# Loading a kernel's first activations by column blocks instead of row blocks

## The chip, the cores and the metric

The kernel runs on one core of a Trainium2 chip. The metric is the device time of one execution in microseconds, as the median of several runs. The core has TensorE (PE), VectorE (DVE), ScalarE (ACT), GpSimd (POOL) and SyncE (SP), and 16 DMA engines. SyncE and ScalarE each issue DMAs on a queue of their own; the 16 engines serve both queues.

## What is computed

The input `x` has 2048 rows of 448 columns in bfloat16. Two branches run over it and are mixed row by row with a gate:

```
g = sigmoid(sum(x * gate_w))                       # one number for each row
a = 2 * Re(C h) + x * Dskip,  h_t = Lam_bar h_(t-1) + B_bar x_t     # a diagonal state-space scan, 448 complex states
b = silu(x @ w1) @ w2                              # w1 is 448 x 1792, w2 is 1792 x 448
out = g * a + (1 - g) * b
```

## The kernel before

**Layout.** Two rows of `x` are taken as one row of 896 values, `x2` (1024 x 896): columns 0 to 447 are the even rows, 448 to 895 the odd ones. TensorE needs `x` with its columns on the partitions; that is `XT`. Columns 0-127, 128-255 and 256-383 fill three column blocks j = 0, 1, 2 of 128 partitions. The remainder, columns 384-447, is half a block (j = 3), and the upper half of the matching tile `XR` holds a second copy of it, so that two matmuls of 64 partitions can run side by side. W1 lies in `W1E` in the same way: row blocks j = 0, 1, 2 and a remainder of 64 rows, `W1E[.., 3, ..]`. This text calls the row blocks W1 block 0, 1 and 2.

**The head.** Nearly all of `XT` is made by transposing DMAs on SyncE's queue, which come late. To start sooner, the first 512 even rows (four row blocks k = 0 to 3 of 128 rows, 512 columns each) come by plain loads into `XH` (a view of `XN`) and are transposed by TensorE: `turn_k(j, k)` (L488) transposes one block of 128 x 128 into PSUM, `turned_k` (L498) and `turned_x` (L504) copy one or several from PSUM into `XT` on VectorE. With them `ffn1_first` (L430) works on the first six blocks of 128 columns of W1: for j = 0, 1, 2 in turn it adds W1's block j times `XT`'s block j into six PSUM banks. Block j = 0 is done in two halves of 256 columns (h = 0 for row blocks 0 and 1, h = 1 for 2 and 3), j = 1 and 2 in one piece of 512. `ffn1_first` is a generator: at each `yield` the code that drives it puts transposes between its matmuls. After it the remainder j = 3 follows (`ffn1_rem`, L444), then silu on ScalarE (L452), and from there the long steady part (`pair`, `lanes`, L362), which runs through the rest of both branches.

**What sets the order.** Every engine runs its instructions in the order of the program. `Tracker` puts a wait before an instruction for each buffer it reads or writes that another engine or a DMA has not finished; the names in `reads` and `writes` are these buffers. A DMA counts as landed when all 16 of its parts have landed. Loads go by `ld` (L226), on the queue of the engine that is named. The first loads are, in order:

- SyncE: row block 0, columns 0-255 (`XA0`); half of W1 block 0; row block 2, columns 0-383 (`XA2`); W1 block 1; two rows for the scan's coefficients (`log_dt`, `Lambda_re`); columns 384-511 of row blocks 2 and 3 (`XB1`); then W1's remainder and its further columns.
- ScalarE: row block 1, columns 0-255 (`XA1`); the other half of W1 block 0; row block 3, columns 0-383 (`XA3`); columns 256-511 of row blocks 0 and 1 (`XB0`); `Lambda_im`; W1 block 2; a table load; then W1's remainder and its further columns.

SyncE then waits for both pieces of W1's remainder (`gE`) before it issues the transposing DMAs. While the head runs, the three rows of coefficients are transposed by four small matmuls (`mm_cols`, L469) and go through a chain of small operations on VectorE and ScalarE; the copies of block j = 3 into `XT` (L504) and `XR` (L568) stand behind the first links of that chain on VectorE.

TensorE begins with 20 matmuls on a constant (`warm`, L478).

Of the kernel before, what the change touches and what calls it, by code (L numbers as in the profile page):

```python
# [11 lines left out]
BF16 = DT.bfloat16  # L12
# [138 lines left out]
def gated_mix(nc, A_x, A_Lambda_re, A_Lambda_im, A_B_re, A_B_im, A_C_re, A_C_im, A_log_dt,  # L151
              A_Dskip, B_x, B_w1, B_w2, gate_w, out):
    with ExitStack() as ctx:
        E = ctx.enter_context
        T = Tracker(nc, ctx)

        def sb(name, shape, dtype):
            return E(nc.sbuf_tensor(name, list(shape), dtype))
# [4 lines left out]
        XT = sb("XT", [128, 8, NK], BF16)  # L163
# [7 lines left out]
        XR = sb("XR", [128, NK], BF16)  # L171
# [17 lines left out]
        ID = sb("ID", [128, 128], BF16)  # L189
# [31 lines left out]
        ps = E(nc.psum_tensor("ps", [128, 8, 512], F32))  # L221
# [3 lines left out]
        def ld(eng, dst, src, key, group=None):  # L225
            return T.dma(eng, lambda e: e.dma_start(dst, src), writes=[key], group=group)  # L226
# [2 lines left out]
            return T.dma("sp", lambda e: e.dma_start_transpose(dst, src), reads=reads,  # L229
                         writes=[key, *also], group=group)  # L230

        XE = [(["XTe000", "XTe001", "XTe010", "XTe011", "XTe02"], ["XTe03"]), (["XTe1"], ["XTer1"])]
        XO = [([f"XTo{h}"], [f"XTr{h}"]) for h in range(2)]

        def swap_xr(eng, h, odd):
# [4 lines left out]
            else:  # L240
                T.op(eng, lambda e: e.tensor_copy(XR[64:128, hs], XT[0:64, 3, hs]), reads=XE[h][1],
                     writes=[f"XR{h}a"])
# [8 lines left out]
            return v.rearrange("(o n) -> o n", o=1)  # L251

        XH = XN[:, 0:8 * D].rearrange("p (k c) -> p k c", k=4)
        XA = ["XA0", "XA1", "XA2", "XA3", "XB0", "XB1"]
        FA, FB = 768, 1280
        x0 = x2[0:512, 0:512].rearrange("(k p) c -> p k c", p=128)

        def ld_w(eng, j, f0=0, f1=FA, key=""):
            ld(eng, W1E[:, j, f0:f1], B_w1[j * 128:(j + 1) * 128, f0:f1], f"W1Ej{j}{key}")

        def ld_row(eng, i, v):
            ld(eng, R[i:i + 1, 0:D], row(v), f"R{i}", gR if i < 2 else gR2)
# [9 lines left out]
                          B_w1[384:448, FA:].rearrange("p (n c f) -> p n c f", n=2, c=2)[:, :, c, :], f"W1Es{c}")  # L272
            return ld(eng, W1E[p, 3, 0:384], B_w1[384:448, 384 * c:384 * c + 384], f"W1Er{c}")

        for k, eng in enumerate(("sp", "act")):
            ld(eng, XH[:, k, 0:256], x0[:, k, 0:256], XA[k])
        for c, eng in enumerate(("sp", "act")):
            ld_w(eng, 0, 384 * c, 384 * c + 384, c)
        for k, eng in ((2, "sp"), (3, "act")):
            ld(eng, XH[:, k, 0:384], x0[:, k, 0:384], XA[k])  # L280
        ld_w("sp", 1)
        ld("act", XH[:, 0:2, 256:512], x0[:, 0:2, 256:512], XA[4])
        for i, (eng, v) in enumerate((("sp", A_log_dt), ("sp", A_Lambda_re), ("act", A_Lambda_im))):
            ld_row(eng, i, v)
        ld_w("act", 2)
        ld("sp", XH[:, 2:4, 384:512], x0[:, 2:4, 384:512], XA[5])
        T.op("act", lambda e: e.activation(JK[:, 0:1], HP[:, :], AF.Exp), reads=["HP"], writes=["JK0"])
        gE = [ld_wr(eng, c, False) for c, eng in enumerate(("sp", "act"))]
        ld_w3("sp", 0, 2, FA, FB, "d")
# [20 lines left out]
        for i, src in enumerate((A_B_re, A_B_im)):  # L310
# [15 lines left out]
             writes=["IOTA"])  # L326
# [9 lines left out]
        def nxt():  # L336
            n_bank[0] += 1
            return BANKS[(n_bank[0] - 1) % len(BANKS)]
# [7 lines left out]
        def rem_keys(odd, h, p):  # L346
            return (XO if odd else XE)[h][1] if (p is UP) == bool(odd) else [f"XR{h}{'b' if odd else 'a'}"]

# [48 lines left out]
        def ff(fb):  # L397
            i, c = fb // 2, fb % 2
            return i + 3 * c if i < 3 else i + 3 + 2 * c if i < 5 else i + 5 + 2 * c

        def wj(fb):
            i, c = fb // 2, fb % 2
            return [f"W1Ej0{c}", "W1Ej1", "W1Ej2"] if i < 3 else ["W1Ed0", "W1Ed2"] if i < 5 else ["W1Ee0", "W1Ee1"]

        def w1(fb):
            return lambda p, j: W1E[p, j, ff(fb) * 128:(ff(fb) + 1) * 128] if j < 3 else \
                W1E[p, j, fb // 2 * 128:(fb // 2 + 1) * 128]

        def rem_ffn1(odd, h, fb):
            return [*[f"W1E{'r' if fb < 6 else 's'}{c}" for c in range(2)], *rem_keys(odd, h, LO), *rem_keys(odd, h, UP)]  # L410
# [6 lines left out]
        def ffn1_pair(c, fb, p=None):  # L417
            odd, h = c // 2, c % 2
            banks = at(p) if p is not None else [nxt(), nxt()]
            return (*[(banks[i], odd, h, w1(fb + i)) for i in range(2)],  # L420
                    wj(fb) + wj(fb + 1) + (XO if odd else XE)[h][0], rem_ffn1(odd, h, fb),
                    lambda: ffn1_act(c, fb, banks[0], 2))

        def ffn1_first():
            banks = [nxt() for _ in range(NF1)]
            for j, h in ((0, 0), (0, 1), (1, None), (2, None)):
                c = slice(0, 512) if h is None else slice(256 * h, 256 * h + 256)
                for n, fb in enumerate((0, 2, 4, 1, 3, 5)):
                    bank = banks[fb]
                    T.op("pe", lambda pe, fb=fb, bank=bank, j=j, h=h, c=c: pe.matmul(  # L430
                        ps[:, bank, c], W1E[:, j, ff(fb) * 128:(ff(fb) + 1) * 128], XT[:, j, c],
                        start=(h == 0), stop=(h == 0), skip_group_check=(h != 0)),
                        reads=[f"W1Ej{j}" if j else f"W1Ej0{fb % 2}"] + (
                            ["XTe02"] if j == 2 else [f"XTe0{j}{h}"] if h is not None else [f"XTe0{j}0", f"XTe0{j}1"]),
                        writes=[f"ps{bank}"])
                    if (j, h, n) in ((0, 0, 3), (0, 0, 5), (1, None, 2), (1, None, 5)):
                        yield
            yield banks

# [10 lines left out]
        def ffn1_act(c, fb, bank, n=1):  # L450
            a = AT[c % 2]
            T.op("act", lambda e: e.activation(a[:, fb:fb + n, :], ps[:, bank:bank + n, :], AF.Silu),  # L452
                 reads=[f"ps{bank + i}" for i in range(n)], writes=[f"AT{c % 2}_{fb + i}" for i in range(n)])
# [26 lines left out]
            T.op("pe", mm, writes=[f"ps{b}"])  # L480

        warm(NWARM, 5)
        PB = (6, 7, 6, 7)
        xp = [ps[:, b, 0:256].bitcast(BF16) for b in PB]

        def turn_k(j, k, b=None):
            b = PB[j] if b is None else b
            T.op("pe", lambda pe: pe.transpose(  # L488
                ps[:, b, 0:256].bitcast(BF16)[:, k * 128:(k + 1) * 128], XH[:, k, j * 128:(j + 1) * 128], ID[:, :]),
                reads=[XA[k if j < 2 or (j == 2 and k > 1) else 4 + k // 2], "ID"], writes=[f"ps{b}"])  # L490

        def turn_x(j, i):
            for k in (2 * i, 2 * i + 1):
                turn_k(j, k)

        def turned_k(j, k, b):
            c = slice(128 * k, 128 * k + 128)
            T.op("dve", lambda e: e.tensor_copy(XT[:, j, c], ps[:, b, 0:256].bitcast(BF16)[:, c]),  # L498
                 reads=[f"ps{b}"], writes=[f"XTe0{j}{k // 2}" + ("" if k % 2 else "a")])

        def turned_x(j, i=None, b=None):
            c, key = (slice(0, 512), f"XTe0{j}") if i is None else (slice(256 * i, 256 * i + 256), f"XTe0{j}{i}")
            b = PB[j] if b is None else b
            T.op("dve", lambda e: e.tensor_copy(XT[:, j, c], ps[:, b, 0:256].bitcast(BF16)[:, c]),  # L504
                 reads=[f"ps{b}"], writes=[key])

        for k in range(2):
            turn_k(0, k, 6 - k)
            turned_k(0, k, 6 - k)
        turn_x(1, 0)  # L510
        turned_x(1, 0)
        warm(2, 4)
        first = ffn1_first()
        next(first)
        for k in (2, 3):
            turn_k(0, k, k + 4)
            turned_k(0, k, k + 4)
        next(first)
        for k in (2, 3):
            turn_k(1, k, 6)  # L520
        turned_x(1, 1, 6)
        rd()
        next(first)
        T.op("pe", mm_cols, reads=["R0", "R1", "R2", "Rd", "ID"], writes=["pv"])
        T.op("dve", lambda e: e.tensor_copy(
            PV[:, :, :], ps[:, 7, 256:288].rearrange("p (t c) -> p t c", c=8)[:, :, 0:4]),
            reads=["pv", "ps7"], writes=["PV"])
        for i in range(2):
            turn_x(2, i)
        turned_x(2)  # L530
        next(first)
        for i in range(2):
            turn_x(3, i)
# [24 lines left out]
        def pact(o, a, f, ra, scale=1.0, bias=0.0):  # L558
# [6 lines left out]
        ptt("ar", col("dt"), LRE, ALU.mult, ["dt", "PV"])  # L565
        pact("mag", col("ar"), AF.Exp, ["ar"])
        turned_x(3)
        T.op("dve", lambda e: e.tensor_copy(XR[64:128, 0:512], xp[3][0:64, :]), reads=["ps7"], writes=["XR0a"])  # L568
        T.op("act", lambda e: e.activation(JK[:, 0:1], HP[:, :], AF.Silu), reads=["HP"], writes=["JK0"])
        ld_b(GWB, gate_w, "GW")  # L570
        ld_b(DB, A_Dskip, "DB")
# [9 lines left out]
            reads=["f2"] + SGN, writes=["f2s"])  # L581
# [55 lines left out]
        def xblock(b):  # L637
            v = XN[:, 4 * b * D:4 * (b + 1) * D].rearrange("p (k c) -> p k c", k=4) if b > 1 else \
                XH[:, :, b * D:(b + 1) * D]
            return v, [*(XA if b < 2 else []), *([f"XN{b // 2}"] if b else [])]  # L640

# [24 lines left out]
        for n in (32, 64):  # L666
            T.op("dve", lambda e, n=n: e.tensor_copy(GD[n:2 * n, :, :], GD[0:n, :, :]), reads=["GW", "DB"],
                 writes=["GW", "DB"])
# [7 lines left out]
             writes=["BTz"] + BTK[2:4])  # L676
# [174 lines left out]
        def bu_even(pt, h, p=None, q=None):  # L851
# [4 lines left out]
            def done():  # L856
# [5 lines left out]

            return (*[(b[i], 0, h, lambda p, j, i=i: bt(p, j, m + i)) for i in range(2)], BTK[0:2] + XE[h][0],
                    BTK + XE[h][0] + rem_keys(0, h, LO) + rem_keys(0, h, UP), done)

# [5 lines left out]
        def bu3_even(p, q):  # L871
            b = at(p)

            def done():
# [7 lines left out]

            return (*[(b[h], 0, h, lambda p, j: bt(p, j, 6)) for h in range(2)], ["BR"] + XE[0][0] + XE[1][0],
                    ["BR"] + rem_keys(0, 0, LO) + rem_keys(0, 1, UP), done)
# [278 lines left out]
        f = ffn1(2)  # L1163
# [100 lines left out]
```

## Time and profile before

| | before |
|---|---|
| runs, us | 136.57, 136.66, 136.79 (median 136.66) |
| profiled execution, span from first to last instruction, us | 135.2 |
| the same execution's whole time | not given by the page; the median of the runs is 1.46 us above the span |
| TensorE matmul busy | 131.8 us, 97% |
| VectorE, ScalarE, GpSimd busy | 115.6, 93.8, 15.9 us |
| granted TensorE clock | 1.000 |
| DMA moved | 11.78 MB, most of it in the first third |

In the chain of work that ended last, TensorE has 94% of the span. Matmuls are pipelined and their ends are modelled, so starts are the better marks. An engine that sits idle costs time only where that chain passes through it.

### The profile page before, as it was taken

Reading aid. Unit: us, or ns where it says so; the run is one execution under the profiler, and the core shown is the slowest. Engines: PE = TensorE matmul, PEld = TensorE weight load, DVE = VectorE, ACT = ScalarE, POOL = GpSimd, SP = SyncE. Lnnn points to the kernel's source line nnn. Section 1 sums busy time; section 2 is a strip of 40 time slices with the busy share of each in tenths; the row PEclk is TensorE's granted clock in tenths of the full one; section 3 lists DMA queues with packets and bytes.
Section 4 is the critical chain, followed back from the end, with each engine's and each line's share of the span. In section 5 each row is a group of like instructions: output and inputs, shape, how many; then the busy total and the mean of one; then the engine's idle time right before and its main releaser. Section 6 shows DMA issues by size and latency. Waiting matters only on the chain.

```text
span 135.2 us, 2632 instructions
## 1 busy us (share of the span) xinstructions
PE 131.8 (97%) x1072; PEld 65.4 (48%) x1073; DVE 115.6 (86%) x154; ACT 93.8 (69%) x146; POOL 15.9 (12%) x32
## 2 busy tenths in 40 slices
PE   7899999999999999999999999999999999999993
PEld 7444444444444554444445544445555555555552
DVE  1369999917899798999999999999999999994554
ACT  0459888899939999769999597797114437879200
POOL 7108349650000000000000000000000000000000
DMA  4999979898997220000222000000000000322123
GB/s 110 259 275 176 125 140 264 165 323 248 259 188 119 53 63 0 0 0 0 55 47 58 5 0 0 0 5 0 0 0 0 0 0 5 102 91 79 68 80 124
DMA packets 24736, 11.78 MB, mean 87 GB/s; under 512 B 16851, under 2 KB 24214, under 8 KB 24726
## 3 DMA queue, kind: packets, MB, share of 16 engines
q1 hardware_dynamic: 22996, 10.43, 33.4%
q10 hardware_dynamic: 1730, 1.20, 3.1%
q8 instruction: 8, 0.13, 0.4%
q14 instruction: 2, 0.02, 0.0%
HBM read 5.34 MB, written 1.84 MB: 53 GB/s over the span
## 4 chain that ended last, share of the span: by engine, by line
PE 94%; DMA 2%; DVE 1%; SPq 1%; issue 0%
PE ps L362 44%; PE ps L796 16%; PE ps L811 16%; PE ps L1049 15%; PE ps L430 3%; DMA XN<-in_A_x_dram 2%; PE ps L488 1%; DVE TMPS L1073 1%; SPq L226 1%; PE ps L444 1%; PE ps L469 0%
## 5 line engine op out<-in xcount | busy, mean ns | idle before, releaser
L362 PE MATMUL ps<-XT,W1E 64*128 64x512 bf16 x325 | 41.3, 376 | 0.0
L452 ACT ACTIVATE AT<-ps 128x1024 bf16<-128x1024 f32 x28 | 28.2, 1020 | 7.4 <-PE ps L362 7.2
L362 PEld LDWEIGHTS ps<-XT,W1E 64*128 64x128 bf16 x325 | 16.9, 94 | 19.1 <-ACT AT L452 0.3
L362 PE MATMUL ps<-XT,BT 64*128 64x512 bf16 x156 | 22.4, 376 | 0.0
L811 PE MATMUL ps<-W,AT 64*128 64x448 bf16 x224 | 21.5, 349 | 0.0
L796 PE MATMUL ps<-W,AT 128*128 128x448 bf16 x112 | 21.4, 353 | 0.0
L796 PEld LDWEIGHTS ps<-W,AT 128*128 128x128 bf16 x112 | 10.9, 98 | 10.5 <-issue 0.4
L811 PEld LDWEIGHTS ps<-W,AT 64*128 64x128 bf16 x224 | 10.9, 94 | 10.4
L840 ACT ACTIVATE BT<-ps,GT 128x448 bf16<-128x448 f32 x8 | 5.1, 634 | 13.2 <-PE ps L796 13.2
L896 DVE SCALAR_TENSOR_TENSOR HS<-VE,P,ps 128x512 bf16<-128x512 bf16 (+1 forms) x13 | 9.6, 781 | 3.8 <-PE ps L362 3.8
L362 PEld LDWEIGHTS ps<-XT,BT 64*128 64x128 bf16 x156 | 8.1, 94 | 9.4 <-DVE HS L896 0.4
L940 DVE TENSOR_TENSOR_SCAN G<-P,Q 128x1024 f32<-128x1024 f32 (+1 forms) x6 | 11.4, 1922 | 0.0
L1049 PE MATMUL ps<-CO,VE 128*128 128x448 bf16 (+2 forms) x63 | 11.1, 332 | 0.0
L1049 PE MATMUL ps<-CO,HS 128*128 128x448 bf16 x56 | 11.1, 352 | 0.0
L362 PE MATMUL ps<-XR,W1E 64*128 64x512 bf16 x25 | 9.2, 376 | 0.0
L1049 PEld LDWEIGHTS ps<-CO,VE 128*128 128x128 bf16 x63 | 6.0, 98 | 4.8
L1049 PEld LDWEIGHTS ps<-CO,HS 128*128 128x128 bf16 x56 | 5.5, 98 | 5.1
L893 DVE TENSOR_TENSOR Q<-G,COS 128x2048 bf16<-128x2048 f32 (+1 forms) x4 | 7.0, 1756 | 0.1
L893 DVE TENSOR_TENSOR Q<-G,SIN 128x2048 bf16<-128x2048 f32 (+1 forms) x4 | 7.0, 1752 | 0.0
L858 ACT ACTIVATE VE<-ps 128x1024 bf16<-128x1024 f32 x6 | 6.1, 1020 | 1.2 <-PE ps L362 1.2
L860 ACT ACTIVATE ps<-VE,P 128x1024 f32<-128x1024 bf16 x6 | 6.7, 1118 | 0.2
L896 DVE SCALAR_TENSOR_TENSOR VE<-HS,P,FP 128x512 bf16<-128x512 bf16 (+1 forms) x7 | 6.6, 977 | 0.1
(124 smaller groups left out, 181.0 us busy)
## 6 DMA issues: line engine op xcount, KB each, us to landing
W<-in_B_w_dram SPq DMA_DIRECT2D x2, 784.0 KB, 6.3
XN<-in_A_x_dram SPq DMA_DIRECT2D x1, 896.0 KB, 5.5
out_dram<-OT SPq DMA_DIRECT2D x8, 112.0 KB, 1.7
out_dram<-TMPS SPq DMA_DIRECT2D x7, 112.0 KB, 1.7
HS<-HS SPq DMA_DIRECT2D x4, 128.0 KB, 2.3
XN<-in_A_x_dram SPq DMA_DIRECT2D x1, 384.0 KB, 3.6
W1E<-in_B_w_dram SPq DMA_DIRECT2D x1, 256.0 KB, 5.6
W1E<-in_B_w_dram ACTq DMA_DIRECT2D x1, 256.0 KB, 5.6
```

The source lines that it names most:

```text
L362: ins = pe.matmul(ps[:, bank, :], w(p, j), xh(odd, h, j, p), start=start and j == js[0], stop=stop and j == js[-1], skip_group_check=seeded)
L430: T.op("pe", lambda pe, fb=fb, bank=bank, j=j, h=h, c=c: pe.matmul(ps[:, bank, c], W1E[:, j, ff(fb) * 128:(ff(fb) + 1) * 128], XT[:, j, c] ...
L452: T.op("act", lambda e: e.activation(a[:, fb:fb + n, :], ps[:, bank:bank + n, :], AF.Silu), reads=[f"ps{bank + i}" for i in range(n)], wri ...
L796: ins = pe.matmul(ps[:, bank, 0:D], a[:, fb, q * 128:(q + 1) * 128], W2[:, ff(fb), :], start=(first and fb == 0), stop=(fb == NFB - 1), sk ...
L811: ins = pe.matmul(ps[:, bank, 0:D], a[p, fb, q * 128:(q + 1) * 128], W2[p, ff(fb), :], start=(start and fb == 0), stop=(not start and fb = ...
L840: T.op("act", lambda e: e.activation(bs(tile), ps[:, bank, 0:D], AF.Copy, scale=sc), reads=[f"ps{bank}", "GT2" if h else "GRI"], writes=ks)
L858: T.op("act", lambda e: e.activation(VE[:, m:m + 2, hs], ps[:, b[0]:b[0] + 2, :], AF.Copy), reads=[f"ps{i}" for i in b], writes=vs)
L860: T.op("act", lambda e: e.activation(ps[:, o[0]:o[0] + 2, :], VE[:, m:m + 2, hs], AF.Copy, scale=c1("lr", pt)), reads=vs + ["lr"], writes= ...
L893: T.op("dve", lambda e: e.tensor_tensor(o, a, b, op), reads=reads, writes=writes)
L896: T.op("dve", lambda e: e.scalar_tensor_tensor(o, a, s, b, ALU.mult, ALU.add), reads=reads, writes=writes)
L940: T.op("dve", lambda e: e.tensor_tensor_scan(G[:, c, w], rb, Q1[:, c, w], init, ALU.mult, ALU.add), reads=[f"Q1{c}", "rr", f"G{c}"], write ...
L1049: ins = pe.matmul(ps[:, bank, c], state(kt, odd, m), CO[:, m, c], start=False, stop=(m == YB[-1]), skip_group_check=True)
```

## The change

The first 512 even rows are no longer loaded mainly by row blocks, but by column blocks of all four row blocks: columns 0-127 (in two DMAs of two row blocks each, one on each queue), columns 128-255 and columns 256-511 (one DMA each, both on ScalarE's queue). W1 block 2 moves from ScalarE's queue to SyncE's, behind block 1. The transposes follow: all four of a column block together, block j = 0 with two copies of 256 columns, blocks 1, 2 and 3 with one copy of 512 columns each. The `yield` places in `ffn1_first` move accordingly: block 1 is transposed ahead of the last three matmuls of block 0, block 2 in the middle of block 1's six matmuls, and block 3 in the middle of block 2's, where it stood ahead of all six before. The coefficients' small matmuls stand behind block 1's six matmuls. What is computed does not change.

```diff
-        for k, eng in enumerate(("sp", "act")):
-            ld(eng, XH[:, k, 0:256], x0[:, k, 0:256], XA[k])
+        for i, eng in enumerate(("sp", "act")):
+            ld(eng, XH[:, 2 * i:2 * i + 2, 0:128], x0[:, 2 * i:2 * i + 2, 0:128], XA[i])
         for c, eng in enumerate(("sp", "act")):
             ld_w(eng, 0, 384 * c, 384 * c + 384, c)
-        for k, eng in ((2, "sp"), (3, "act")):
-            ld(eng, XH[:, k, 0:384], x0[:, k, 0:384], XA[k])
         ld_w("sp", 1)
-        ld("act", XH[:, 0:2, 256:512], x0[:, 0:2, 256:512], XA[4])
+        ld("act", XH[:, :, 128:256], x0[:, :, 128:256], XA[2])
+        ld_w("sp", 2)
+        ld("act", XH[:, :, 256:512], x0[:, :, 256:512], XA[3])
         for i, (eng, v) in enumerate((("sp", A_log_dt), ("sp", A_Lambda_re), ("act", A_Lambda_im))):
             ld_row(eng, i, v)
-        ld_w("act", 2)
-        ld("sp", XH[:, 2:4, 384:512], x0[:, 2:4, 384:512], XA[5])
...
-                    if (j, h, n) in ((0, 0, 3), (0, 0, 5), (1, None, 2), (1, None, 5)):
+                    if (j, h, n) in ((0, 1, 2), (1, None, 2), (1, None, 5), (2, None, 2)):
                         yield
...
-        PB = (6, 7, 6, 7)
+        PB = (6, 6, 7, 6)
...
-        for k in range(2):
-            turn_k(0, k, 6 - k)
-            turned_k(0, k, 6 - k)
-        turn_x(1, 0)
-        turned_x(1, 0)
+        for i in range(2):
+            for k in (2 * i, 2 * i + 1):
+                turn_k(0, k, 6 + i)
+            turned_x(0, i, 6 + i)
         warm(2, 4)
         first = ffn1_first()
         next(first)
-        for k in (2, 3):
-            turn_k(0, k, k + 4)
-            turned_k(0, k, k + 4)
+        for i in range(2):
+            turn_x(1, i)
+        turned_x(1)
         next(first)
-        for k in (2, 3):
-            turn_k(1, k, 6)
-        turned_x(1, 1, 6)
+        for i in range(2):
+            turn_x(2, i)
+        turned_x(2)
         rd()
         next(first)
         T.op("pe", mm_cols, reads=["R0", "R1", "R2", "Rd", "ID"], writes=["pv"])
         T.op("dve", lambda e: e.tensor_copy(
             PV[:, :, :], ps[:, 7, 256:288].rearrange("p (t c) -> p t c", c=8)[:, :, 0:4]),
             reads=["pv", "ps7"], writes=["PV"])
-        for i in range(2):
-            turn_x(2, i)
-        turned_x(2)
         next(first)
         for i in range(2):
             turn_x(3, i)
...
-        T.op("dve", lambda e: e.tensor_copy(XR[64:128, 0:512], xp[3][0:64, :]), reads=["ps7"], writes=["XR0a"])
+        T.op("dve", lambda e: e.tensor_copy(XR[64:128, 0:512], xp[3][0:64, :]), reads=["ps6"], writes=["XR0a"])
```

The parts left out are the names of the buffers, and the removal of `turned_k`.

More of the change, by code (lines that the diff above doesn't have):

```diff
@@ L230, in ldt @@
                          writes=[key, *also], group=group)
-        XE = [(["XTe000", "XTe001", "XTe010", "XTe011", "XTe02"], ["XTe03"]), (["XTe1"], ["XTer1"])]
+        XE = [(["XTe000", "XTe001", "XTe01", "XTe02"], ["XTe03"]), (["XTe1"], ["XTer1"])]
         XO = [([f"XTo{h}"], [f"XTr{h}"]) for h in range(2)]
@@ L253, in gated_mix @@
         XH = XN[:, 0:8 * D].rearrange("p (k c) -> p k c", k=4)
-        XA = ["XA0", "XA1", "XA2", "XA3", "XB0", "XB1"]
+        XA = ["XA0", "XA1", "XA2", "XA3"]
         FA, FB = 768, 1280
@@ L432, in ffn1_first @@
                         start=(h == 0), stop=(h == 0), skip_group_check=(h != 0)),
-                        reads=[f"W1Ej{j}" if j else f"W1Ej0{fb % 2}"] + (
-                            ["XTe02"] if j == 2 else [f"XTe0{j}{h}"] if h is not None else [f"XTe0{j}0", f"XTe0{j}1"]),
+                        reads=[f"W1Ej{j}" if j else f"W1Ej0{fb % 2}", f"XTe0{j}" if h is None else f"XTe0{j}{h}"],
                         writes=[f"ps{bank}"])
-                    if (j, h, n) in ((0, 0, 3), (0, 0, 5), (1, None, 2), (1, None, 5)):
+                    if (j, h, n) in ((0, 1, 2), (1, None, 2), (1, None, 5), (2, None, 2)):
                         yield
@@ L489, in turn_k @@
                 ps[:, b, 0:256].bitcast(BF16)[:, k * 128:(k + 1) * 128], XH[:, k, j * 128:(j + 1) * 128], ID[:, :]),
-                reads=[XA[k if j < 2 or (j == 2 and k > 1) else 4 + k // 2], "ID"], writes=[f"ps{b}"])
+                reads=[XA[min(j + 1, 3) if j else k // 2], "ID"], writes=[f"ps{b}"])
         def turn_x(j, i):
@@ L494, in turn_x @@
                 turn_k(j, k)
[L496 to L499, printed above, removed]
         def turned_x(j, i=None, b=None):
```

## The prediction

> **What bounds the kernel now.** I read the chain of work that ended last first, since it says which part of the span a change of loads can reach at all.
>
> ```profile
> 1.70 3.25 DMA XN<-in_A_x_dram
> ...
> 5.00 0.39 PE ps L488 x2
> 5.39 0.22 PE ps L430 x2
> ...
> 8.48 1.29 PE ps L430 x6
> 9.78 0.75 PE ps L444 x6
> 10.53 31.76 PE ps L362 x294
> ```
>
> From 5.00 us to 132.7 us every piece is TensorE work. So nothing behind the head has slack: if the first remainder matmul (L444; L441 in the changed kernel) starts later, the end comes later by the same amount. I therefore forecast one number, the start of that matmul, 9.71 us now. The timeline of TensorE over the head shows where it stands idle:
>
> ```profile
> 3.77 0.71 PE L430 MATMUL ps<-XT,W1E 128*128 128x256 bf16 x4
> 5.00 0.39 PE L488 MATMUL ps<-ID,XN 128*128 128x128 bf16 x2 [0.53 <-DMA XN<-in_A_x_dram]
> ...
> 8.32 1.46 PE L430 MATMUL ps<-XT,W1E 128*128 128x512 bf16 x6
> 9.71 0.39 PE L444 MATMUL ps<-XT,W1E 64*128 64x512 bf16 x1
> ```
>
> One DMA wait of 0.53 us, and after it only short waits for copies. The table by stretches (its last three fields are granted clock, DMA share and GB/s) and the list of DMA issues say what the head's loads are limited by:
>
> ```profile
> 2.00:2.50 0.50, 0.50 (x8) 0.50 (x6) 0.00 (x0) 0.00 (x0) 0.43 (x2) 1.00 1.01 209
> 3.00:3.50 0.50, 0.50 (x8) 0.44 (x5) 0.24 (x2) 0.00 (x0) 0.50 (x1) 1.00 1.06 341
> 5.00:5.50 0.50, 0.50 (x4) 0.26 (x4) 0.23 (x2) 0.20 (x1) 0.00 (x0) 1.00 1.00 339
> ```
>
> ```profile
> W1E<-in_B_w_dram SPq DMA_DIRECT2D x1, 192.0 KB, 4.2
> W1E<-in_B_w_dram ACTq DMA_DIRECT2D x1, 192.0 KB, 4.1
> XN<-in_A_x_dram SPq DMA_DIRECT2D x2, 64.0 KB, 3.2
> XN<-in_A_x_dram ACTq DMA_DIRECT2D x1, 128.0 KB, 4.5
> ```
>
> The 16 DMA engines are full from 2.0 us on, so what lands when is decided by order and share, not by when an instruction is issued. Three facts come from the trace's packet and landing records. (a) A packet takes 18 ns at 256 B, 27 at 512 B, 36 at 768 B, 46 at 1024 B, 65 at 1536 B; a DMA here has one packet per row piece, spread evenly over 16 engines. (b) While W1's block 1 (SyncE, 1536 B) and x's last 512 B piece (ScalarE) are both in flight, 4.25 to 4.75 us, 60 packets of the one and 70 of the other start: the queues take turns packet by packet, not byte by byte. (c) One of the 16 parts comes last by far: W1 block 2 has its middle part at 6.0 and its last at 7.37 us, and TensorE waits for the last.
>
> **The loads, worked out.** Per DMA engine, in packets x ns. Before, SyncE's queue carries 8x27 (x), 8x36 (W1), 8x36 (x), 8x65 (W1 block 1), 16x18 (x): 48 packets, 1.60 us. ScalarE's carries 8x27, 8x36, 8x36, 16x27, 8x65 (W1 block 2): 48 packets, 1.75 us. Both lists hold only what the head needs, and both end together: 1.85 (first packet) + 3.35 = 5.20 us by count; the last parts landed at 7.37 and 7.57. So the last landing is some 2.1 us behind the count (first packets of a region that take up to 0.5 us, the last part, the landing itself). The same check on x's 512 B piece, 40 packets on each side, 4.54 by count and 6.66 landed, gives 2.1 again; that is the value I use.
>
> After, ScalarE's queue carries 16x18 (x columns 0-127, upper row blocks), 8x36 (W1), 32x18 (columns 128-255), 32x27 (columns 256-511): 88 packets, 0.29+0.29+0.58+0.86 = 2.02 us. SyncE's carries 16x18, 8x36, 8x65, 8x65: only 40 packets, 1.62 us. Then it goes on with W1 pieces that are used much later: 4x36, 16x46, 8x27, 8x46, together 36 packets, 1.47 us. The change thus makes x cost 0.29 us more per engine (2.02 against 1.73, from the 256 B pieces), puts all of x but 64 KB on one queue, and lets the other queue's long packets, needed or not, pass one for one.
> - Columns 128-255 end as ScalarE's 56th packet. 56 of SyncE's have gone too: 1.62 + 0.14 + 12x0.046 = 2.31. Count 1.85 + 1.16 + 2.31 = 5.32, last landing 7.4 us.
> - Columns 256-511 end as the 88th; all 76 of SyncE's have gone: 1.85 + 2.02 + 3.09 = 6.96, last landing 9.1 us.
>
> **TensorE's path, step by step.** The first loads land about 0.15 us later (32 packets of 18 ns in place of 16 of 27), so the first L430 starts at 3.85, not 3.77. Nine 256-column matmuls in a row (0.11 each) then end at 4.9: the 0.53 us wait is gone, worth that much if nothing else came late. But the next instruction transposes columns 128-255, and TensorE goes in order: it stands until 7.4, a wait of 2.5 us; behind it are the last three 256-column matmuls, all 12 of 512 columns and the rows' transposes for the scalar chain. From there: four transposes 4x0.055 = 0.22 plus 0.16 until the last one's result, the copy of 512 columns 0.42 (timeline: 0.42 for this shape), 0.12 for the two hand-overs; three 256-column matmuls lie under the copy. Block 1's matmuls start at 7.4 + 0.05 + 0.92 = 8.4, three of 512 columns (0.216 each) end at 9.0, and columns 256-511 land at 9.1. From that landing: 0.05 + four transposes 0.22 + three matmuls 0.65 + the four 4-column ones 0.10 + three 0.65 + four transposes 0.22 = 1.89. Now one wait is new: before, six matmuls (1.3 us) lay between these last transposes and L444, after only three (0.65). The copies of the fourth block and of XR end 0.91 us after the transposes' results now (8.48 to 9.39), so the matmul waits for VectorE: 1.89 + 0.16 + 0.91 + 0.04 = 3.0 us behind the landing. Start 9.1 + 3.0 = 12.1 against 9.71, that is 2.35 us later. A landing of columns 256-511 at 6.7 us would be even.
>
> **What is moved and costs nothing.** VectorE has three copies fewer (about 0.3 us); it waits for TensorE there. Log_dt, Lambda_re and Lambda_im need not be early, since their transposes stand behind the first 512-column matmuls. The SyncE transposes wait for both W1 remainder pieces, of which ScalarE's is now queued behind x: about 9.3 against 8.01 us. Their first result is read at 15.8 us, 6 us after L444, and is there by 14.2; the reader shifts by 2.35, so 1.3 is covered, and with no cover at all it would cost 1.3 us. ScalarE's table load follows its issues and is needed only for the scalar chain. PSUM bank 6 is reused by blocks 0, 1 and 3, whose copies are long done by then.
>
> **The sum.** The page gives the profiled execution as a span of 135.2 us; the median of the runs, 136.66, has 1.46 us around it, which I leave as it is. 136.66 + 2.35 = 139.0 us.
>
> **Rivals.**
> - *x gets a better share.* If a queue kept an engine for 16 packets at a time, columns 256-511 would have only 2.72 of SyncE's 3.09 us ahead, 128-255 1.76: landings 6.9 and 8.7, start 11.7, 138.6 us. With equal time for both queues 256-511 would land at 1.85 + 4.04 + 2.1 = 8.0, start 11.0, 138.0 us. For it: fact (b) is 60 to 70, read from a half microsecond with mixed sizes. Against it: block 1 and the 512 B piece, 8 and 16 packets, ended in this order (middle parts 5.2 and 5.4), as by turns. Chance 0.2. The Trainium skill (DMA: Bandwidth & Descriptors, "Queues, rings and completion order") has an engine change queues only after a whole packet of typically 9 to 17 descriptors, and by that rule 138.6 would be the sum; the counts above do not show such runs, so I keep the turn by turn.
> - *The other side: faster.* If the last part's lag (some 1.2 of the 2.1 us, between middle and last part) is an accident of the profiled run and the queues share time, columns 256-511 land at 6.8 or sooner. Then TensorE sets the pace: 3.85 + 24 matmuls (1.32 + 2.59) + 12 transposes 0.66 + 0.10 + copy waits of 0.4 and 0.45 = 9.37, a gain of 0.34: 136.3 us. It decides below 6.7 us. For it: the early loads (2.85 and 3.02 us) show no lagging part. Against: from 4.96 us on every DMA of the head has one. With turns but no lag it would still be 7.9, and 137.8 us. Chance of a gain 0.1.
> - *The clock falls in the wait.* The 128-column matmuls before 3.5 us start 0.107 us apart, the 256-column ones from 4.1 on 0.110, so the array ran at half rate until some four microseconds. If a wait of 2.5 us takes it back, the 12 matmuls of 512 columns cost up to 2.6 us more; with half of that, 140.3 us. Against: the wait of 0.53 us changed nothing, but no longer one is in the trace. Chance 0.07. The Trainium skill (TensorE: Matmul & The Clock Gate, "What's actually happening") lets the clock fall after an idle window of about 3.4 us, longer than this wait; by that rule nothing is added.
>
> **How the numbers follow.** The forecast, turns packet by packet with the lag, gets 0.6 and 139.0 us; better share 0.2 (138.0 to 138.6); gain 0.1; about even 0.03; the clock 0.07. The range takes in the forecast with its landings 1 us sooner or 1.5 later, and the better share: 137.2 to 140.5, with the gains and the worst of the clock left out. 0.2% (0.27 us) is about what this kernel's measurement can tell: faster 0.1, same 0.03, slower 0.87.
>
> **What would show it.** In the profile after: on TensorE a DMA wait of some 2.5 us before the second group of transposes, released by x; a second, short one before columns 256-511; SyncE's two W1 blocks landing before columns 128-255; the first remainder matmul near 12 us, idle before it on XR's copy; from there the same work at the same pace. It is wrong if that matmul starts before 10 us, or if the columns land before W1's block 2.

## The result and the profile after

The changed kernel takes 137.91 us in the median (137.21 to 138.10) against 136.66: the ratio of the runs is 1.0085, 95% interval 1.0062 to 1.0108, which is 1.16 us (0.85 to 1.48). Slower, as forecast, but half as much as forecast (2.35), and inside the range. The profiled execution has a span of 136.8 us against 135.2.

The chain of work that ended last, start and length in us, is no longer TensorE alone between 5 us and the end:

```profile
1.30 2.90 DMA W1E<-in_B_w_dram
...
4.25 2.10 PE ps L428 x9
...
6.70 0.44 DVE XT L496
7.13 0.14 issue
7.27 0.81 PE ps L428 x3
...
10.15 0.42 DVE XT L496
10.58 0.03 issue
10.61 0.43 DVE XR L556
11.04 0.14 issue
11.17 0.82 PE ps L441 x6
12.00 31.82 PE ps L360 x294
```

VectorE's copies have come into it at two places, and behind 12.00 us it is what it was (31.82 us for the same 294 matmuls, 31.76 before). The timeline of TensorE has the waits in brackets:

```profile
4.25 2.10 PE L428 MATMUL ps<-XT,W1E 128*128 128x256 bf16 x9 [0.28 <-DMA W1E<-in_B_w_dram]
...
7.27 0.81 PE L428 MATMUL ps<-XT,W1E 128*128 128x512 bf16 x3 [0.28 <-DVE XT L496]
...
9.95 0.81 PE L428 MATMUL ps<-XT,W1E 128*128 128x512 bf16 x3
11.17 0.37 PE L441 MATMUL ps<-XT,W1E 64*128 64x512 bf16 x1 [0.41 <-DVE XR L556]
```

In the kernel before, the weights of the first three matmuls of 512 columns give that mark, since the timeline of TensorE merges these matmuls with the ones ahead of them (PEld is the weight load, which overlaps the matmul):

```profile
6.46 0.33 PEld L430 LDWEIGHTS ps<-XT,W1E 128*128 128x128 bf16 x3 [0.20 <-DMA W1E<-in_B_w_dram]
```

Two marks carry the comparison. The first matmul of 512 columns (W1 block 1) starts at 7.27 us, before at 6.46: 0.81 later. The first remainder matmul starts at 11.17, before at 9.71: 1.46 later. So 0.65 us are lost between the two marks, 3.90 us in place of 3.25, and 0.81 ahead of them. The 2.5 us wait for x that the forecast was built on is not there. The loads came much sooner than worked out:

```profile
W1E<-in_B_w_dram SPq DMA_DIRECT2D x2, 192.0 KB, 3.4
...
XN<-in_A_x_dram ACTq DMA_DIRECT2D x1, 256.0 KB, 4.5
...
XN<-in_A_x_dram ACTq DMA_DIRECT2D x1, 128.0 KB, 3.6
```

The last figure is us from issue to landing: columns 128-255 landed at 5.47 us, columns 256-511 at 6.86. The table by stretches (last two fields: DMA share and GB/s) shows the DMA engines about as full as before:

```profile
3.00:3.50 0.50, 0.50 (x6) 0.28 (x5) 0.00 (x0) 0.00 (x0) 0.50 (x1) 1.00 0.96 272
...
5.00:5.50 0.50, 0.50 (x4) 0.32 (x3) 0.00 (x0) 0.03 (x1) 0.00 (x0) 1.00 1.09 363
```

### The profile page after: what moved, and what is told of

It reads as the page before. It is cut to its first block, busy times and chain, and to the rows that moved or that the text cites. A ratio compares the mean times of both kernels' runs of the same rounds, so it can differ in the third digit from the quotient of the medians.

```text
span 136.8 us, 2624 instructions
## 1 busy us (share of the span) xinstructions
PE 132.8 (97%) x1072; PEld 66.0 (48%) x1073; DVE 115.3 (84%) x151; ACT 93.7 (68%) x146; POOL 15.9 (12%) x32
## 4 chain that ended last, share of the span: by engine, by line
PE 94%; DMA 2%; DVE 2%; issue 0%; SPq 0%
PE ps L360 43%; PE ps L784 16%; PE ps L799 15%; PE ps L1037 15%; PE ps L428 3%; DMA W1E<-in_B_w_dram 2%; DVE TMPS L1061 1%; DVE XT L496 1%; PE ps L441 1%; PE ps L485 1%; SPq L226 0%; DVE XR L556 0%; PE ps L466 0%
## 5 line engine op out<-in xcount | busy, mean ns | idle before, releaser
L496 DVE COPY XT<-ps 128x512 bf16<-128x512 bf16 (+1 forms) x5 | 1.8, 371 | 6.0 <-PE ps L485 5.9
```

## The experiments

Times are medians; each ratio is to the kernel before on the same chip, with its 95% interval.

### Both kernels again

No edit.

> The kernel before, unchanged, profiled a second time. Two things from the first profile are to be told apart as fixed or accidental: the one part of 16 that lands 0.7 to 1.4 us after the others in every load of the head from 4.96 us on, and the array's clock rising at about 4.0 us. If the late part belongs to the kernel, W1 block 2 lands its last part near 7.4 again with a middle part near 6.0; if it was an accident, near 6.4. If the clock's rise belongs to the kernel, the 256-column matmuls start 0.11 us apart again; if it is a matter of luck, some of them 0.21 apart. Span 135.0 to 135.5 us either way, because TensorE has slack of at most 0.5 us against the loads.

Span 135.2 us again, the first remainder matmul at 9.73 us. W1 block 2's middle part came at 6.14 and its last at 7.00, the last x piece at 6.32 and 7.41: the lagging part is there again, 0.9 to 1.1 us, a little less than the first time. The 256-column matmuls were 0.11 us apart from 3.9 us on.

> The changed kernel, unchanged, profiled a second time. Theory 1 (the wait of half a microsecond on W1 block 0 keeps the clock at half rate): the first nine 256-column matmuls are 0.213 us apart again whenever a wait of 0.4 us or more stands ahead of them, and the first remainder matmul starts near 11.2 us. Theory 2 (the forecast's: the order of x and W1 on the queues makes x late): the clock plays no part, columns 128-255 and 256-511 land at 5.5 and 6.9 us again and TensorE's first remainder matmul starts at 11.2 whatever the first matmuls' pace. If W1 block 0 lands by 3.8 this time and the clock is up by 4.3, theory 1 gives a start near 10.5 and a span near 136.0 us.

Span 136.8 us again, the first remainder matmul at 11.22, yet by another road. The array ran at full rate from 4.6 us on, and the nine matmuls were done by 5.2; this time the wait was for x (chain of work):

```profile
1.84 4.42 DMA XN<-in_A_x_dram
6.27 0.05 issue
6.32 0.41 PE ps L485 x4
```

One of the 16 parts of columns 128-255 came at 6.27 us, the middle one at 4.96 as before. Block 1 started at 7.32, 0.05 from the first profile. Neither theory alone holds: half rate in the one run and a late part in the other gave the same start.

### Filling TensorE's wait

```diff
-        warm(2, 4)
+        warm(6, 4)
```

> Six filler matmuls instead of two between the first transposes and the first L428 matmul, so that TensorE is not idle while it waits for W1 block 0 (0.107 us each at half rate, the last ends near 4.2 us). Theory 1 (idle time there holds the clock at half rate): the clock rises near 4.2 us, nine matmuls at 0.11 in place of 0.213 us, 0.9 us sooner; of that some is lost again to the landing of columns 128-255 (5.5 us): first remainder matmul 10.5 in place of 11.2 us, time 0.6 to 0.7 us under the changed kernel, 137.2 us. Theory 2 (only the loads' order counts): no gain, 137.9 us, or up to 0.2 us more from the filler.

137.92 us, ratio 1.0081 (1.0052 to 1.0109): no gain. The chain shows TensorE at work without a break from the first instruction, and the nine matmuls still at 0.213 us:

```profile
0.82 2.29 PE ps L475 x20
3.11 0.43 PE ps L485 x4
3.54 0.64 PE ps L475 x6
4.18 1.92 PE ps L428 x9
```

Full rate came at 6.1 us. So the wait ahead of L428 is not what keeps the array at half rate; theory 1 of this run falls.

### The order after block 1, undone by halves and whole

Block 3's transposes ahead of all six block-2 matmuls:

```diff
-                    if (j, h, n) in ((0, 1, 2), (1, None, 2), (1, None, 5), (2, None, 2)):
+                    if (j, h, n) in ((0, 1, 2), (1, None, 2), (1, None, 5)):
...
-        next(first)
         for i in range(2):
             turn_x(3, i)
```

> The transposes of column block 3 stand ahead of all six matmuls of block 2, as in the kernel before, and not in their middle; all loads as in the changed kernel. If the wait of 0.41 us for the XR copy ahead of the first remainder matmul is due to that place alone, 0.2 to 0.4 us come back: 137.6 us. If instead VectorE's chain of small operations holds the copies (they stand behind it), the wait stays and the time is 137.9 us. The clock plays no part in it.

137.72 us, 1.0065 (1.0042 to 1.0087): at most a little. The wait ahead of the remainder fell from 0.41 to 0.20 us (between the marks 3.69 us). What is left of it is VectorE's: its copies of block 3 stand behind links of the coefficients' chain, which ran at 9.44 us here and at 7.99 in the kernel before. And ScalarE then was late; its timeline:

```profile
9.93 1.28 ACT L556 ACT_TABLE_LOAD   x1
11.23 0.20 ACT L556 ACTIVATE JK<-HP 128x1 bf16<-128x1 f32 x1
11.34 1.92 ACT L449 ACTIVATE AT<-ps 128x1024 bf16<-128x1024 f32 x2
```

The table for silu is loaded behind the two exponentials of the coefficients, which wait for the small matmuls (8.63 us here). The first silu started the moment the table was in, 11.34, though its matmuls had started at 10.61, and TensorE's next group, waiting for those PSUM banks, started at 12.40 and not 12.14.

The small matmuls ahead of block 2's transposes, block 3's left in the middle:

```diff
         turned_x(1)
-        next(first)
-        for i in range(2):
-            turn_x(2, i)
-        turned_x(2)
         rd()
         next(first)
         T.op("pe", mm_cols, ...)
...
+        for i in range(2):
+            turn_x(2, i)
+        turned_x(2)
+        next(first)
         next(first)
         for i in range(2):
             turn_x(3, i)
```

> The changed kernel with the coefficients' small matmuls back ahead of block 2's transposes, but block 3 still transposed in the middle of block 2's matmuls. If the two places add: 0.2 us before the small matmuls comes back, the wait for the XR copy (0.4 us) stays, 137.6 us. If the wait for XR is shorter because VectorE's chain is done early, 137.3 us. If the moved small matmuls cost through ScalarE's Silu table load behind them, which the first silu waits for, the first silu starts at once behind its matmuls.

137.62 us, 1.0074 (1.0050 to 1.0099). The wait for XR stayed at 0.41 us with the small matmuls early, so it comes from the place of block 3's transposes. The table was in by 10.2 us, and the first silu waited for its matmuls.

Both together:

> The order of TensorE's and VectorE's work after block 1 as in the kernel before: the coefficients' small matmuls ahead of the transposes of block 2, the transposes of block 3 ahead of all six matmuls of block 2; all loads and the transposes by whole column blocks as in the changed kernel. Theory 1 (two thirds of a microsecond of the loss is this order: 0.2 us for the coefficient rows, 0.45 us for the XR copy): from the first block-1 matmul to the first remainder matmul 3.25 us, as before, in place of 3.90; and ScalarE's Silu table load is early again, so nothing is lost behind it: 137.3 us. Theory 2 (the loads make the loss, the order only follows): 3.9 us stays, 137.9 us.

> The changed kernel's loads and transposes with the order of the kernel before after block 1, measured and profiled again, since its first profile had the array at half rate until 7.9 us, longer than in any other. Theory 1 (loads cost little once the order is back): 136.7 to 137.1 us again, and in a profile with the clock up by 5 us the first block-1 matmul near 6.9 and the first remainder matmul near 10.1 us. Theory 2 (the loads cost 0.5 us or more): 137.2 us or above.

136.98 us, 1.0017 (0.9997 to 1.0036), and again 136.97 us, 1.0027 (1.0004 to 1.0049). Timeline of TensorE in the second:

```profile
9.08 1.46 PE L428 MATMUL ps<-XT,W1E 128*128 128x512 bf16 x6
10.47 0.39 PE L441 MATMUL ps<-XT,W1E 64*128 64x512 bf16 x1
```

No wait in brackets, and 3.23 us from the first 512-column matmul (7.24) to the remainder. Some 0.8 to 0.9 us come back, where each half alone gave 0.15 to 0.3 that the intervals do not separate from none. With block 3 alone moved, the table load came last; with the small matmuls alone moved, XR's copy did.

### The order alone, in the kernel before

Loads and blocks 0 and 1 as before, the changed order of block 2, small matmuls and block 3:

```diff
-                    if (j, h, n) in ((0, 0, 3), (0, 0, 5), (1, None, 2), (1, None, 5)):
+                    if (j, h, n) in ((0, 0, 3), (0, 0, 5), (1, None, 2), (1, None, 5), (2, None, 2)):
...
         turned_x(1, 1, 6)
+        next(first)
+        for i in range(2):
+            turn_x(2, i)
+        turned_x(2)
         rd()
         next(first)
         T.op("pe", mm_cols, ...)
...
-        for i in range(2):
-            turn_x(2, i)
-        turned_x(2)
         next(first)
         for i in range(2):
             turn_x(3, i)                # now in the middle of block 2's matmuls
```

> One part of the change alone, put into the kernel before: its loads by row blocks and its transposes of blocks 0 and 1 stay, but block 2 is transposed in the middle of block 1's six matmuls, the coefficients' small matmuls stand behind all six, and block 3 is transposed in the middle of block 2's, as in the changed kernel. Theory 1 (this order makes most of the loss, whatever the loads): 3.9 us from the first 512-column matmul to the first remainder matmul in place of 3.25, and the time 0.65 to 0.9 us above the kernel before: 137.3 to 137.6 us. Theory 2 (the order costs only behind late loads): within 0.2 us of 136.66.

137.33 us, 1.0056 (1.0036 to 1.0077), 0.76 us above the kernel before. Timeline of TensorE:

```profile
9.19 0.81 PE L430 MATMUL ps<-XT,W1E 128*128 128x512 bf16 x3
10.41 0.37 PE L444 MATMUL ps<-XT,W1E 64*128 64x512 bf16 x1 [0.41 <-DVE XR L569]
```

Block 1 started at 6.50, as in the kernel before, and the remainder 3.91 us later, with the changed kernel's own 0.41 us wait. With loads that nobody touched, the order costs some two thirds of the whole loss (0.76 of 1.16 us, both with wide intervals). The array ran at half rate until 6 us in this profile, and block 1 was not late for it.

### How the queues share, and what passes x

W1 blocks 1 and 2 in packets of 768 B:

```diff
-        ld_w("sp", 1)
+        for c in range(2):
+            ld("sp", W1E[:, 1, 384*c:384*c+384], B_w1[128:256, 384*c:384*c+384], ...)
```

> W1 blocks 1 and 2 in two DMAs each, on the same queue and in the same place, so that their packets are 768 B and not 1536 B; all else as in the changed kernel. What is asked is how the two queues share a DMA engine, read from the landing of columns 128-255 (middle part 5.0 us in both profiles of the changed kernel). Theory 1 (the forecast's: one packet of each queue in turn): ScalarE's 32 packets of 256 B then pass beside shorter packets and end about 0.5 us sooner, middle part near 4.5 us, and W1 block 2 later than 5.7. Theory 2 (the queues share the engine's time, or its bytes): the same landings within 0.2 us. First remainder matmul, by theory 1, up to 0.5 us sooner where the clock is up; by theory 2 between 10.7 and 11.3 us as before.

Columns 128-255 came with the middle part at 4.57 us (4.83 to 5.05 in the ten other profiles that load them in this place): theory 1's number. But the edit also makes two loads of one, and the second half of W1 block 1 is issued 0.5 us behind the first. Between 3.75 and 4.25 us, 397 of x's 512 packets start beside only 26 of SyncE's. So x may have gained from a gap between the halves as much as from the shorter packets; the run does not tell the two apart. W1 block 2 has the middle of its 32 parts at 6.2 us (5.7 in one load) and the last at 7.57 (5.96 and 6.30). The first remainder matmul started at 11.13; the array was at half rate until 6.5, and the one execution took 138.31 us.

W1's later pieces on SyncE's queue held back:

```diff
+        T.wait_all("sp", [gHold])       # columns 256-511 have landed
         gE = [ld_wr(eng, c, False) for c, eng in enumerate(("sp", "act"))]
```

> The changed kernel with SyncE's later W1 pieces (remainder and further columns) issued only once columns 256-511 have landed. Only the landing of columns 256-511 is asked for; the transposing DMAs come later with it, so the time may be up to 1 us worse. Theory 1 (the forecast's: these 36 packets per engine pass x one for one): columns 256-511 land up to 1 us sooner, the middle part near 5.5 to 5.8 in place of 6.45 to 6.5 us. Theory 2 (in the changed kernel these pieces begin to move only at 5.75 us, when most of x has gone): the same landing within 0.25 us.

Columns 256-511 landed with the middle part at 6.43 and the last at 7.13 us, as without the hold (6.45 and 6.86, 6.53 and 7.05): theory 2. The one execution took 138.08 us. In the packet records of the changed kernel these pieces, issued from 3.4 us on, first move at 5.75.

### Columns 128-255 on both queues, and versions that might win

```diff
+        gX = T.group()
+        ld("sp", XH[:, 0:2, 128:256], x0[:, 0:2, 128:256], "XA2x", gX)
+        ld("act", XH[:, 2:4, 128:256], x0[:, 2:4, 128:256], XA[2], gX)
         ld_w("sp", 1)
-        ld("act", XH[:, :, 128:256], x0[:, :, 128:256], XA[2])
```

> Columns 128-255 in two DMAs of two row blocks, one on each queue, both ahead of W1 block 1; the order of the engines' work as in the changed kernel. Theory 1 (the late landing of columns 128-255, 5.4 to 6.3 us, is the other part of the loss): they land by 4.8 us, the first block-1 matmul starts near 6.3 in place of 7.3 us, and the first remainder matmul, 3.9 us behind it or 3.0 us behind columns 256-511 (6.9 us), near 10.2: 136.9 to 137.1 us. Theory 2 (the half-rate clock holds TensorE, not the load): block 1 starts near 7.0 whenever the clock rises only at 6 us, 137.7 us.

138.35 us, 1.0118 (1.0097 to 1.0140): slower still. Block 1 did start sooner in the profile (6.56), but W1 block 1 landed at 6.34 in place of 5.0 to 5.3, and TensorE then stood for columns 256-511:

```profile
7.68 0.40 PE L487 MATMUL ps<-ID,XN 128*128 128x128 bf16 x4 [0.32 <-DMA XN<-in_A_x_dram]
```

The profile is of the fastest of its six runs, so it does not show the whole of that loss.

> Both: columns 128-255 shared between the queues ahead of W1 block 1, and the order after block 1 as in the kernel before. If the two parts are independent, they add: block 1 near 6.3 us, first remainder matmul near 9.6, time 136.3 to 136.6 us, level with the kernel before or just under it. If columns 256-511 (6.9 us) bind, the remainder starts near 9.9 and the time is 136.8. If the clock is the cause, 137.3 us.

With the order of the kernel before after block 1 as well: 137.28 us, 1.0041 (1.0027 to 1.0056). In the profile, again of the fastest run, block 1 started at 6.21, and the next wait was the coefficient rows:

```profile
7.36 0.24 PE L468 MATMUL ps<-ID,R 128*128 128x4 bf16 x4 [0.34 <-DVE R L462]
```

With the order of the kernel before after block 1, and columns 128-255 on one queue as in the change, block 1 copied in two halves:

```diff
-            turn_x(1, i)
-        turned_x(1)
+            for k in (2 * i, 2 * i + 1):
+                turn_k(1, k, 6 + i)
+            turned_x(1, i, 6 + i)
```

> The changed kernel's loads, the order of the kernel before after block 1, and block 1 copied in two halves of 256 columns from two PSUM banks, the first under the second pair of transposes. In the profiles the first block-1 matmul starts 0.55 us behind the last 256-column one's start, waiting for the 0.42 us copy. If that copy is on the path, 0.1 to 0.15 us come off: 136.8 us against 136.9 to 137.0 with one copy. If W1 block 1 or the clock is what holds block 1, nothing.

136.82 us, 1.0019 (1.0002 to 1.0037): the best of these, not to be told from one copy, and still not under the kernel before. In its profile VectorE waits for the rows as well:

```profile
6.92 0.17 DVE L461 COPY R<-R 3x64 bf16<-3x64 bf16 x1 [0.78 <-DMA R<-in_A_Lambda_re_dram]
```

So, in the next run, the rows were issued ahead of W1 block 2 and of columns 256-511:

> As the run with block 1 copied in halves and the kernel before's order after block 1, and the three coefficient rows issued earlier: two ahead of W1 block 2 on SyncE's queue, one ahead of columns 256-511 on ScalarE's. In the profile of that run the small matmuls waited 0.31 us for the rows (landed by 6.9 us, in the kernel before by 6.1). Theory 1 (what the loads still cost with the order back is mostly these rows, queued behind more bytes): the rows land by 6.0, the 0.3 us wait is gone, and the time is 136.4 to 136.6 us, level with the kernel before or just under it. Theory 2 (x's own late columns cost it): columns 256-511 or W1 block 2 hold TensorE in place of the rows, 136.8 us.

137.00 us, 1.0031 (1.0010 to 1.0051): no gain. The rows landed by 5.24, but W1 block 2 came at 7.12 and columns 256-511 at 7.88, and x held TensorE in their place (theory 2):

```profile
7.93 0.40 PE L487 MATMUL ps<-ID,XN 128*128 128x128 bf16 x4 [0.18 <-DMA XN<-in_A_x_dram]
```

No version ran faster than the kernel before.

## Why the prediction was right or wrong, point by point

- **What bounds it: right.** The first remainder matmul started 1.46 us later and the last VectorE instruction 1.52 us later (134.22 against 132.70). The times of these two profiled executions, 138.03 and 136.73 (the kernel before's second profile, of the same span), differ by 1.30: what lies around the span is not quite constant, 1.2 to 1.5 us.
- **The landing of columns 256-511: the step that failed.** Forecast 9.1 us, measured 6.86 and 7.05. Of the 2.1 to 2.2 us, 1.47 are W1's later pieces, which I let pass x one for one; the run that held them back shows that they do not. Without them the count is 1.85 + 2.02 + 1.62 = 5.49, and the middle part landed 0.95 to 1.05 behind it, as in the kernel before (6.1 against 5.20). The rest is the last part: I added the 1.2 us lag of the first profile, and here it was 0.4 to 0.5.
- **The landing of columns 128-255: failed with it.** Forecast 7.4, measured 5.47 and 6.27. Here 0.69 us are the later pieces. Without them the turns give 1.85 + 1.16 + 1.62 = 4.63, with 0.9 for the middle part 5.5, and it came at 4.96 to 5.02. Equal time for both queues, the rival, gives 1.85 + 2 x 1.16 + 0.9 = 5.1. So fact (b), one packet in turn, read off half a microsecond, is 0.5 us out, and equal time is nearer; but what the rule is stays open. The packet records show no steady share: between 4.25 and 4.50 us (second profile) 159 packets of 256 B start beside 14 of 1536 B, which take 89 ns on average and not 65. By count those 14 are nearly the last of W1 block 1 (110 of its 128 had started by 4.25), so SyncE's queue seems to have had little ready; why block 2 did not move sooner was not tried. The last part's lag was 0.45 and 1.3 us, against the 1.2 that I added.
- **The wait for x, and with it the forecast's signs: wrong.** TensorE waited for columns 128-255 not at all in the first profile and 0.99 us in the second, in place of 2.5, and for columns 256-511 in neither. Columns 128-255 landed before W1 block 2 (5.47 against 5.96, 6.27 against 6.30), which I had named as a sign of being wrong.
- **TensorE's path behind the landings: in part right.** From the first of block 1's transposes to block 1 itself 1.00 us were measured (second profile) against 0.92 forecast. The first L428 was put at 3.85 and came at 4.25, for one late part of W1 block 0 (4.20 us, the other 15 by 3.62), and at 3.89 the second time. The wait for XR was put at 0.45; the gap ahead of the remainder grew by 0.48 (0.79 in place of 0.31 from the last matmul's start). Worked out by the forecast's own terms, block 1's start to the remainder is 3.60 us, and 3.90 were measured. With the measured landings these terms put the remainder at 10.0 and 10.8 us, where 11.17 and 11.22 were measured; in the first profile the array at half rate makes 0.8 of the difference. That the time fell inside the range is thus in part luck: landings forecast too late were partly offset by costs that the forecast did not have.
- **"Need not be early": wrong.** I priced the moved small matmuls at nothing. They cost 0.2 us where they stand, waiting for VectorE's copy of the rows, which now stands behind block 2's copy. And ScalarE's table load hangs on them: once XR's wait was gone, the first silu waited for it. Together with XR's wait the order costs 0.76 us (0.49 to 1.05), which the forecast had at 0.45.
- **The sum.** Order 0.76; loads and transposes by column blocks, with the order back, 0.23 to 0.37 (one of the two intervals takes in zero): 1.0 to 1.1, the 1.16 measured within its interval. I had 1.9 for the loads. What is left of the loads' cost is not one wait: after the rows were moved, x came last, and after x was moved, W1 and the rows did.
- **The rivals.** The equal share gave 138.0 us, next to the measured time, but by a landing at 8.0 that was 6.9; the time is a coincidence of that mechanism with an order that costs more than I said. The better share in runs of 16 packets (landing 8.7) is farther off. The Trainium skill's rule (DMA: Bandwidth & Descriptors, "Queues, rings and completion order") is not settled by that: the 138.6 us that I set beside it hold W1's later pieces and the lag as well, and the packet records here do not name the engine, so that runs on one engine cannot be told from them. The gain's condition, a landing below 6.7, was nearly met, and did not help: columns 256-511 were not what TensorE waited for.
- **The clock.** I let it fall in a wait. In the one longer wait that came, 0.99 us, it did not fall; a wait of 2.5 us did not come. But it had often not risen. Half rate ended between 3.9 and about 8 us in the 16 profiles of all kernels, in nine of them after 5 us, with either order and either set of loads. How much of the 0.23 to 0.37 us it makes was not separated.

## What to carry to other kernels

Price the order of the work by its own rows, apart from the loads: here the instructions that moved along with a load cost some two thirds of the loss, and the loads and transposes by column blocks, which were the point of the change, a fifth to a third. When a step moves, follow everything that hangs on its result, through to the last engine, a table load among them. And take a lag or a share from one profile as one sample: where the sum rests on it, run the kernel before a second time first.

## What the runs showed of the hardware

- **Half rate despite steady work.** With TensorE busy from 0.82 us on without a break, the 256-column matmuls stayed 0.213 us apart until 6.1 us in one run; in others they were 0.11 apart from 3.9. The granted clock reads 1.00 throughout, so it has to be read from the spacing of the starts. The Trainium skill (TensorE: Matmul & The Clock Gate, "What's actually happening") describes a window of some 3.4 us that runs freely and does not start with the kernel, so that the rise comes at another time in each run; by that rule it would lie before 0.82 + 2 x 3.41 = 7.6 us, an estimate from that page, and 15 of the 16 profiles agree. The sixteenth, at about 8 us, had TensorE idle for 0.8 us ahead of the first L428; another with 0.7 us of idle time there rose at 4.6, so the idle time alone does not explain it. At the other end, four profiles rose at 3.9 to 4.0 us, 3.1 to 3.2 us after the first matmul and so sooner than a whole such window of work.
- **One part of 16.** In the loads of x and W1 issued before 3.4 us, the last part came 0.1 to 1.6 us behind the middle one, in the same kernel differently from run to run (columns 128-255: 0.45 and 1.3 us in the changed kernel's two profiles).
- **Small loads ahead of large ones: one sample.** With three rows of 0.9 KB issued ahead of them, W1 block 2's last part came 1.1 us later than with the rows behind (7.12 against 6.00) and columns 256-511 1.0 us later (7.88 against 6.89). The middle part of W1 block 2 did not move (5.62 against 5.58), so its delay is a late part and may be chance; that of columns 256-511 did (7.05 against 6.30). Why was not tried.
